# Attention by halves of the sequence: two head tiles at a time, column-tiled logits, and an output projection that starts inside the attention

## The chip, the cores and the metric

The kernel runs on one core of a Trainium2 chip. The core has a matrix engine (TensorE, PE in the profile), three elementwise engines (VectorE or DVE, ScalarE or ACT, GpSimd or POOL) and a queue engine (SyncE, SP) that starts transfers. Each engine executes its own instructions in order and waits on semaphores for the others. The time is the device time of one execution in microseconds; lower is better.

## The reference, cut to what matters

Two layers of attention and token MLP run one after the other on one sequence of 2048 positions and 1024 channels. The attention is local: every position looks at eight positions, itself and those 2, 4, ... 14 before it.

```python
def _A_ref(x, wqkv, wo):              # S = 2048, D = 1024, 32 heads of 32 channels
    W, dil = 8, 2
    q, k, v = ...                     # x @ wqkv, by heads
    idx = pos[:, None] - off[None, :] # off = 0, 2, ... 14; masked where idx < 0
    logits = einsum("bhsd,bhswd->bhsw", q, kg) * scale     # kg: k at idx
    attn = softmax(where(mask, logits, -1e9))
    o = einsum("bhsw,bhswd->bhsd", attn, vg)
    return o.reshape(B, S, D) @ wo

def _B_ref(x, w1, b1, w2, b2):        # mixes positions: 2048 -> 3584 -> 2048
    h = layernorm(x)
    u = gelu(einsum("bsd,sf->bdf", h, w1) + b1)
    return transpose(einsum("bdf,fs->bds", u, w2) + b2)

x = x + _A_ref(layernorm(x), wqkv, wo)
x = x + _B_ref(layernorm(x), w1, b1, w2, b2)
x = x + _A_ref(layernorm(x), wqkv, wo)
x = x + _B_ref(layernorm(x), w1, b1, w2, b2)
```

## The kernel before

One **unit** of the attention is one tile of 128 channels (four heads) over all 2048 positions, `t = 0..7`. Its steps are:

- `QK(t)` and `V(t)`: 64 and 32 matmuls of 512 columns; ScalarE copies the sums into `q_buf`, `k_buf`, `v_buf`.
- `products(t)`: VectorE multiplies q with the eight shifted copies of k, 8192 elements a partition for each half of the positions.
- `reduce(t)`: 32 matmuls with a 0/1 matrix `Z` sum the 32 channels of a head. All add into one PSUM tile `lg` of 128 partitions, each matmul filling four of them.
- `softmax1`, `softmax2`: VectorE and ScalarE; the weights go to DRAM (`attn_scr`) and come back spread over the channels (`bcast`, 2 MB for each half).
- `AVp`: VectorE multiplies them with the eight shifted copies of v; `accum` adds the eight, on VectorE, or on TensorE for the last two units.

```python
def reduce(t):
    lg = psum.tile([P, W, SUB], F32, name="lg", tag="lg", bufs=2)
    nc.tensor.matmul(lg[:CP], lhsT=maskL[:W, :], rhs=maskR[:W], start=True, stop=False)
    for hh in range(2):
        for jj in range(JH):
            j = hh * JH + jj
            nc.tensor.matmul(lg[:CP], lhsT=Z[:, ZOFF - H4 * j: ZOFF - H4 * j + CP],
                             rhs=pr_buf[hh][:, :, jj * SUB:(jj + 1) * SUB],
                             start=False, stop=(j == NJ - 1))

def pe_acc(t):
    return t >= ND - 2                     # ND = 8

for t in range(-2, ND + 1):                # a software pipeline over units
    AVp(t - 1, 0); accum(t - 1, 0)
    reduce(t); softmax1(t)
    ...                                    # AVp/accum of half 1, softmax2(t), bcast
    products(t + 1)
    QK(t + 2, ...); V(t + 1)
    load_wqkv(t + 3)
    if t + 1 == ND - 1:
        load_wo(); load_w1(0)
load_w1(1)
```

The output projection `OutProj.run` needs all eight units of a row. It follows the attention, 16 rows of 128 positions, each 16 matmuls, an addition of the residual on VectorE and the LayerNorm for the MLP; the first two rows are begun (seven of eight tiles) in the attention's last step.

```python
for i in range(NS):                        # NS = 16 rows
    self.mm(i, ...)                        # oh (attention out) x wo
    nc.vector.tensor_tensor(xo[:], pyv, xb[:], op=ALU.add)
    nc.sync.dma_start(self.xd[i * P:(i + 1) * P, :], xo[:])
    mv = ln_stats(xo[:])
    ...                                    # ScalarE writes the normalized row into oh
```

At the very start all 16 rows are normalized and transposed into `hT`; the attention begins with the last of them. In the second layer the second MLP step prepares `hT` while it runs.

Of the kernel before, what the change touches and what calls it, by code (L numbers as in the profile page):

```python
# [9 lines left out]
BF = mybir.dt.bfloat16  # L10
# [5 lines left out]
P = 128  # L16
# [8 lines left out]
NEG = -1.0e10  # L25


def build_kernel(ctx, tc, A_x, A_wqkv, A_wo, B_w1, B_b1, B_w2, B_b2, out, n_layers=2, dbg=None,
                 wq_eng="gpsimd"):
# [7 lines left out]
    NJ = S // SUB  # L37
    CP = NJ * H4
    assert CP <= P
    HS = S // 2  # L40
    JH = NJ // 2
    CPH = CP // 2
# [4 lines left out]
    wdma = {"gpsimd": nc.gpsimd, "sync": nc.sync, "scalar": nc.scalar}[wq_eng]  # L47
# [21 lines left out]
    maskR = const.tile([P, W, SUB], BF, name="maskR")  # L69
    eps_t = const.tile([P, 1], F32, name="eps_t")  # L70
# [3 lines left out]
    with tc.tile_pool(name="cbuild", bufs=1) as cb:  # L74
# [7 lines left out]
        mlf = cb.tile([P, CP], F32, name="mlf")  # L82
        nc.gpsimd.memset(mlf[:], 1.0)
        nc.gpsimd.affine_select(out=mlf[:], in_=mlf[:], pattern=[[-1, CP]],
                                compare_op=ALU.is_ge, fill=0.0, base=H4 - 1, channel_multiplier=0)
        nc.vector.tensor_copy(maskL[:], mlf[:])
# [29 lines left out]
    KT_W = HALO_PAD + S  # L116
# [3 lines left out]
    n_qkv = max(2 * S + 5 * KT_W, NF * 512)  # L120
    n_w = 2 * ND * 3 * P
    n_wv = 2 * ND * P
    n_wall = max(n_w + n_wv, NS * 512)
# [5 lines left out]
    R_w = R_wall[:, 0:n_w].rearrange("p (b k g c) -> p b k g c", b=2, k=ND, g=3)  # L129
    R_wv = R_wall[:, n_w:n_w + n_wv].rearrange("p (b k c) -> p b k c", b=2, k=ND)  # L130
# [11 lines left out]
    q_buf = [R_qkv[:, b * S:(b + 1) * S] for b in range(2)]  # L142
    k_buf = [R_qkv[:, 2 * S + b * KT_W: 2 * S + (b + 1) * KT_W] for b in range(2)]
    v_buf = [R_qkv[:, 2 * S + (2 + b) * KT_W: 2 * S + (3 + b) * KT_W] for b in range(3)]

    def zero_halos():
        for b in k_buf + v_buf:
            nc.vector.memset(b[:, 0:HALO_PAD], 0.0)
# [36 lines left out]
    def load_wqkv(t):  # L185
        if t < 0 or t >= ND:
            return
        b = t % 2
        with nc.allow_non_contiguous_dma("weight slice, 256B runs"):
            for g in range(3):  # L190
                nc.sync.dma_start(R_w[:, b, :, g, :], wq_view[:, :, g, t * P:(t + 1) * P])

    def permute_wv(t):
        if t < 0 or t >= ND:
            return
        b = t % 2
        nc.scalar.copy(R_wv[:, b, :, :].rearrange("p k (d h) -> p k d h", h=H4),
                       R_w[:, b, :, 2, :].rearrange("p k (h d) -> p k d h", h=H4))
# [19 lines left out]
    def attention(li, before_last_qk_chunk=None, drain_filler=None):  # L218

        def QK(t, hook=None):  # L220
            if t < 0 or t >= ND:
                return
            b = t % 2
            qT, kT = q_buf[b], k_buf[b]
            QW = min(1024, S)
            units = [(g, c2) for c2 in range(S // QW) for g in (0, 1)]
            for ui, (g, c2) in enumerate(units):
                if hook is not None and c2 == S // QW - 1 and g == 0:
                    hook()
                dst, off = (qT, 0) if g == 0 else (kT, HALO_PAD)  # L230
                pq = mm_tile()
                for n in range(QW // 512):
                    s0 = c2 * QW + n * 512
                    for kt in range(ND):
                        nc.tensor.matmul(pq[:, n * 512:(n + 1) * 512], lhsT=R_w[:, b, kt, g, :],  # L235
                                         rhs=hT[:, kt, s0:s0 + 512], start=(kt == 0), stop=(kt == ND - 1))
                nc.scalar.copy(dst[:, off + c2 * QW: off + (c2 + 1) * QW], pq[:, 0:QW])  # L237

        def V(t):
            if t < 0 or t >= ND:  # L240
                return
            b = t % 2
            vT = v_buf[t % 3]
            QW = min(1024, S)
            for c2 in range(S // QW):
                pq = mm_tile()
                for n in range(QW // 512):
                    s0 = c2 * QW + n * 512
                    for kt in range(ND):
                        nc.tensor.matmul(pq[:, n * 512:(n + 1) * 512], lhsT=R_wv[:, b, kt, :],  # L250
                                         rhs=hT[:, kt, s0:s0 + 512], start=(kt == 0), stop=(kt == ND - 1))
                nc.scalar.copy(vT[:, HALO_PAD + c2 * QW: HALO_PAD + (c2 + 1) * QW], pq[:, 0:QW])

        qkv_pitch = R_qkv.ap[0][0]

        def shifted(buf, col0):
            return bass.AP(buf.tensor, buf.offset + col0, [[qkv_pitch, P], [-DIL, W], [1, HS]])

        def products(t):
            if t < 0 or t >= ND:  # L260
                return
            qT, kT = q_buf[t % 2], k_buf[t % 2]
            for hh in range(2):
                nc.vector.tensor_tensor(pr_buf[hh], qT[:, hh * HS:(hh + 1) * HS].unsqueeze(1).to_broadcast([P, W, HS]),  # L264
                                        shifted(kT, HALO_PAD + hh * HS), op=ALU.mult)
# [3 lines left out]
        def reduce(t):  # L269
            if t < 0 or t >= ND:  # L270
                return
            lg = psum.tile([P, W, SUB], F32, name="lg", tag="lg", bufs=2)
            lg_tiles[t] = lg
            nc.tensor.matmul(lg[:CP], lhsT=maskL[:W, :], rhs=maskR[:W], start=True, stop=False)
            for hh in range(2):
                prod = pr_buf[hh]
                for jj in range(JH):
                    j = hh * JH + jj
                    nc.tensor.matmul(lg[:CP], lhsT=Z[:, ZOFF - H4 * j: ZOFF - H4 * j + CP],  # L279
                                     rhs=prod[:, :, jj * SUB:(jj + 1) * SUB],  # L280
                                     start=False, stop=(j == NJ - 1))

        sm_state = {}

        def softmax1(t):
            if t < 0 or t >= ND:
                return
            lg = lg_tiles.pop(t)
            mx = atp.tile([P, SUB], F32, name="mx")
            nc.vector.tensor_reduce(mx[:CP], lg[:CP].rearrange("p w s -> p s w"), axis=AX.X, op=ALU.max)  # L290
            lm = atp.tile([P, W, SUB], F32, name="lm")
            nc.vector.tensor_tensor(lm[:CP], lg[:CP], mx[:CP].unsqueeze(1).to_broadcast([CP, W, SUB]),
                                    op=ALU.subtract)
            nc.scalar.activation(lm[:CP], lm[:CP], ACT.Exp, scale=scale)
            sm_state[t] = lm

        def softmax2(t):
            if t < 0 or t >= ND:
                return None
            lm = sm_state.pop(t)  # L300
# [5 lines left out]
            scr = attn_scr[t % 2]  # L306
            with nc.allow_non_contiguous_dma("compact attn scatter, 128B runs"):
                for hh in range(2):
                    dst = bass.AP(scr.tensor, hh * H4 * W * HS, [[SUB, JH], [W * HS, H4], [HS, W], [1, SUB]])
                    nc.sync.dma_start(dst, at[hh * CPH:(hh + 1) * CPH])  # L310
                    if dbg is not None and "attn" in dbg and li == 0:
                        nc.sync.dma_start(bass.AP(dbg["attn"].tensor, t * H4 * W * S + hh * HS,
                                                  [[SUB, JH], [W * S, H4], [S, W], [1, SUB]]),
                                          at[hh * CPH:(hh + 1) * CPH])

            def bcast(hh):
                src = bass.AP(scr.tensor, hh * H4 * W * HS, [[0, DH], [W * HS, H4], [1, W * HS]])
                nc.sync.dma_start(ab_of(t, hh), src)

            bcast(0)  # L320
            return lambda: bcast(1)

        def ab_of(t, hh):
            return pr_buf[hh] if t == ND - 1 else ab_buf[hh]

        def AVp(t, hh):
            if t < 0 or t >= ND:
                return
            vT = v_buf[t % 3]
            ab = ab_of(t, hh)  # L330
            nc.vector.tensor_tensor(ab, ab, shifted(vT, HALO_PAD + hh * HS), op=ALU.mult)  # L331

        def pe_acc(t):
            return t >= ND - 2

        def accum(t, hh):
            if t < 0 or t >= ND:
                return
            ab = ab_of(t, hh)
            dst = oh[:, t, hh * HS:(hh + 1) * HS]  # L340
            if not pe_acc(t):
# [15 lines left out]
        zero_halos()  # L357
        for t in range(-2, ND + 1):
            AVp(t - 1, 0)
            accum(t - 1, 0)  # L360
            reduce(t)
            softmax1(t)
            if t == ND - 1:
                b1 = softmax2(t)
                b1()
                AVp(t - 1, 1)
                accum(t - 1, 1)
                if drain_filler is not None:
                    drain_filler()
            else:  # L370
                AVp(t - 1, 1)
                b1 = softmax2(t)
                accum(t - 1, 1)
                if b1 is not None:
                    b1()
            products(t + 1)
            if t + 2 >= 2:
# [234 lines left out]
```

## Time and profile before

| what | before |
|---|---|
| time, median of 4 runs | 1497.69 us (1497.25 to 1498.64) |
| span of the profiled run | 1495.8 us |
| start: LayerNorm and transposes | 0 to 46.4 us |
| attention of layer one, then of layer two | 46.4 to 330.5, and 771.7 to 1056 us |
| output projection | 330.5 to 377.9, and 1056 to 1104.4 us |
| MLP, two steps | 377.9 to 771.7, and 1104.4 to 1495.8 us |

The profile is a trace of one execution. A line of a group names the source line, the engine, the operation and its tiles (out<-in), and how often it ran; then its busy time and mean duration, and the idle time of the engine just before it with what ended it. The string of 40 digits gives the busy tenths of an engine in 40 equal slices of the span. L264 is the multiplication of `products`, L279 the matmuls of `reduce`, L331 the multiplication of `AVp`, L342 to L344 the additions of `accum` on VectorE, L353 those on TensorE, L413 the output projection, L459 and L494 the two MLP steps.

### The profile page before, as it was taken

How to read it: one execution, taken by the hardware profiler on the slowest of the kernel's cores; microseconds unless marked ns; L12 is line 12 of the kernel's file. 1: busy time of each engine (PE TensorE's matmuls, PEld its weight loads, DVE VectorE, ACT ScalarE, POOL GpSimd, SP SyncE). 2: the span in 40 equal slices, each digit the busy share in tenths (PEclk: the TensorE clock that was granted, in tenths of full speed). 3: DMA queues.
4: the chain of work that ended last, by engine and by line, in shares of the span. 5: the costliest groups of instructions: out<-in, count | busy, mean ns of one | idle time of the engine just before them, and what ended most of it. 6: DMA issues, size and time to landing. Idle time of an engine off the chain costs nothing.

```text
span 1495.8 us, 14782 instructions
## 1 busy us (share of the span) xinstructions
PE 1395.8 (93%) x6458; PEld 636.4 (43%) x6544; DVE 619.6 (41%) x633; ACT 326.8 (22%) x345; POOL 41.8 (3%) x53
## 2 busy tenths in 40 slices
PE   3999999489999999999999999965999999999998
PEld 2444444134444444444444444422444444444443
DVE  6439999758100001222234699995750000011111
ACT  4332232014211121222223332310441111100000
POOL 1000000100000000000000000010000000000000
PEclk9999999789999999999999999988999999999999
DMA  8134435864221333414111455286621311224410
GB/s 174 38 124 165 144 126 201 312 231 168 70 83 57 99 71 119 136 44 139 43 50 28 153 188 200 117 288 242 218 100 57 113 57 57 72 70 141 142 48 21
DMA packets 113857, 183.43 MB, mean 123 GB/s; under 512 B 75904, under 2 KB 75904, under 8 KB 109696
## 3 DMA queue, kind: packets, MB, share of 16 engines
q1 hardware_dynamic: 97824, 119.57, 24.0%
q0 software_dynamic: 15968, 62.92, 12.5%
q8 instruction: 51, 0.84, 0.2%
q14 instruction: 14, 0.11, 0.0%
HBM read 163.59 MB, written 18.87 MB: 122 GB/s over the span
## 4 chain that ended last, share of the span: by engine, by line
PE 73%; DVE 21%; DMA 4%; issue 1%; SPq 1%; ACT 0%; DVEq 0%; ACTq 0%
PE mm L459 26%; PE mm L494 26%; PE mm L235 7%; DVE R_att L331 7%; PE mm L413 6%; DVE R_att L264 5%; DVE R_att L342 3%; PE mm L250 3%; DMA R_att<-attn_scr 2%; PE lg L279 2%; PE mm L353 2%; DVE R_att L343 2%; DVE ln_stats L156 1%; DMA attn_scr<-at 1%; DVE sm L302 1%
## 5 line engine op out<-in xcount | busy, mean ns | idle before, releaser
L504 DVE SCALAR_TENSOR_TENSOR xo<-mm,b_sb,xb 128x1024 bf16<-128x1024 f32 x32 | 41.1, 1284 | 689.4 <-PE mm L494 689.4
L235 PE MATMUL mm<-R_hT,R_wall 128*128 128x512 bf16 x994 | 223.6, 381 | 1.7 <-issue 0.2
L459 PE MATMUL mm<-R_oh,R_hT 128*128 128x512 bf16 x1024 | 222.3, 379 | 0.0
L494 PE MATMUL mm<-R_att,R_oh 128*128 128x512 bf16 x878 | 194.1, 379 | 0.9
L494 PE MATMUL mm<-R_att,R_qkv 128*128 128x512 bf16 x876 | 193.8, 379 | 1.1
L264 DVE TENSOR_TENSOR R_att<-R_qkv 128x8192 bf16<-128x8192 bf16 x32 | 141.1, 4419 | 63.7 <-PE lg L279 43.1
L459 PE MATMUL mm<-R_oh,R_wall 128*128 128x512 bf16 x768 | 166.7, 379 | 0.0
L331 DVE TENSOR_TENSOR R_att<-R_att,R_qkv 128x8192 bf16<-128x8192 bf16 x32 | 141.4, 4418 | 47.8 <-DMA R_att<-attn_scr 47.8
L235 PEld LDWEIGHTS <-R_wall 128*128 128x128 bf16 x1024 | 100.6, 98 | 121.1 <-issue 2.2
L459 PEld LDWEIGHTS <-R_hT 128*128 128x128 bf16 x1024 | 100.1, 98 | 120.9
L279 PE MATMUL lg<-R_att,Z 128*128 128x512 bf16 x512 | 118.2, 388 | 30.7 <-DVE R_att L264 30.7
L494 PEld LDWEIGHTS <-R_qkv 128*128 128x128 bf16 x896 | 87.4, 98 | 104.3
L494 PEld LDWEIGHTS <-R_oh 128*128 128x128 bf16 x896 | 87.4, 98 | 103.8
L461 ACT ACTIVATE R_att<-mm,b_sb 128x1024 bf16<-128x1024 f32 x56 | 62.3, 1113 | 307.6 <-PE mm L459 307.5
L459 PEld LDWEIGHTS <-R_wall 128*128 128x128 bf16 x768 | 75.2, 98 | 90.6
L250 PE MATMUL mm<-R_hT,R_wall 128*128 128x512 bf16 x508 | 112.9, 379 | 0.2
L413 PE MATMUL mm<-R_hT,R_oh 128*128 128x512 bf16 x500 | 110.8, 379 | 1.1 <-ACT R_oh L355 0.5
L237 ACT CAST R_qkv<-mm 128x1024 bf16<-128x1024 f32 x64 | 64.7, 1011 | 194.8 <-PE mm L235 194.6
L279 PEld LDWEIGHTS <-Z 128*128 128x128 bf16 x512 | 50.0, 100 | 94.8 <-issue 40.3
L413 PEld LDWEIGHTS <-R_oh 128*128 128x128 bf16 x512 | 50.1, 98 | 61.2 <-issue 1.0
L250 PEld LDWEIGHTS <-R_wall 128*128 128x128 bf16 x512 | 50.1, 98 | 60.4
L353 PE MATMUL mm<-R_att,ident 128*128 128x512 bf16 x126 | 37.6, 462 | 30.3 <-DVE R_att L331 27.6
(65 smaller groups left out, 636.6 us busy)
## 6 DMA issues: line engine op xcount, KB each, us to landing
R_att<-attn_scr SPq DMA_DIRECT2D x32, 2048.0 KB, 9.6
R_hT<-in_B_w_dram POOLq DMA_DIRECT2D x8, 2048.0 KB, 9.6
R_qkv<-in_B_w_dram POOLq DMA_DIRECT2D x4, 3584.0 KB, 16.0
R_oh<-in_B_w_dram POOLq DMA_DIRECT2D x4, 3584.0 KB, 15.0
R_wall<-in_A_wqkv_dram SPq DMA_DIRECT2D x48, 256.0 KB, 3.1
R_wall<-in_B_w_dram POOLq DMA_DIRECT2D x6, 2048.0 KB, 9.5
x_scr<-xo SPq DMA_DIRECT2D x48, 256.0 KB, 2.2
xb<-x_scr SPq DMA_DIRECT2D x48, 256.0 KB, 3.2
```

The costliest lines, as they stand in the source:

```text
L235: nc.tensor.matmul(pq[:, n * 512:(n + 1) * 512], lhsT=R_w[:, b, kt, g, :], rhs=hT[:, kt, s0:s0 + 512], start=(kt == 0), stop=(kt == ND - 1))
L237: nc.scalar.copy(dst[:, off + c2 * QW: off + (c2 + 1) * QW], pq[:, 0:QW])
L250: nc.tensor.matmul(pq[:, n * 512:(n + 1) * 512], lhsT=R_wv[:, b, kt, :], rhs=hT[:, kt, s0:s0 + 512], start=(kt == 0), stop=(kt == ND - 1))
L264: nc.vector.tensor_tensor(pr_buf[hh], qT[:, hh * HS:(hh + 1) * HS].unsqueeze(1).to_broadcast([P, W, HS]), shifted(kT, HALO_PAD + hh * HS), ...
L279: nc.tensor.matmul(lg[:CP], lhsT=Z[:, ZOFF - H4 * j: ZOFF - H4 * j + CP], rhs=prod[:, :, jj * SUB:(jj + 1) * SUB], start=False, stop=(j == ...
L331: nc.vector.tensor_tensor(ab, ab, shifted(vT, HALO_PAD + hh * HS), op=ALU.mult)
L342: nc.vector.tensor_tensor(ab[:, 0:W:2, :], ab[:, 0:W:2, :], ab[:, 1:W:2, :], op=ALU.add)
L353: nc.tensor.matmul(po[:, n * CH:(n + 1) * CH], lhsT=ident[:], rhs=ab[:, w, c0:c0 + CH], start=(w == 0), stop=(w == W - 1))
L413: nc.tensor.matmul(py[:, d0:d0 + 512], lhsT=oh[:, t, i * P:(i + 1) * P], rhs=wo_sb[:, t, d0:d0 + 512], start=(t == 0), stop=(t == ND - 1))
L459: nc.tensor.matmul(pu[:, n * 512:(n + 1) * 512], lhsT=w1t[:, k, f4 * P:(f4 + 1) * P], rhs=h2_rhs(k, n * 512), start=(k == 0), stop=(k == N ...
L461: nc.scalar.activation(gT[:, ft, :], pu[:, 0:D], ACT.Gelu_apprx_tanh, bias=b1_sb[:, ft:ft + 1], scale=1.0)
L494: nc.tensor.matmul(py[:, n * 512:(n + 1) * 512], lhsT=w2t[:, k, s4 * P:(s4 + 1) * P], rhs=gT[:, k, n * 512:(n + 1) * 512], start=(k == 0), ...
```

## The change

The change makes a unit of **two** tiles over **half** of the positions: units 0 to 3 are the four pairs of tiles in the first half, units 4 to 7 the same pairs in the second. It has five parts.

1. The first four units need only the first eight rows of `hT`. The attention starts after these, and the other rows are normalized and transposed between its first projections (`pre_unit_hooks`).
2. The logits of units 0 and 1 are reduced inside the projections of the next unit (`early`), to start VectorE's chain sooner.
3. `reduce` uses column tiling: 32 matmuls with 32 columns each, on four column groups of the array, so that four may run side by side.
4. When unit 3 is done, the first half of the attention's output is complete. Its eight output rows are projected inside the last unit (`drain_filler`), with the residual added on TensorE by an identity matmul and the sum taken from PSUM by ScalarE (`act_evac`). Only the last unit's accumulation is left to TensorE.
5. The weights of Q and K have one buffer for a pair of tiles, loaded in runs of 512 bytes instead of 256. The first two w1 loads wait for the last unit (a two-element copy makes them do so). The 14 positions of k and v that the second half needs from the first are kept in a small `stash`.

```diff
+        def unit_tiles(U):
+            u, p = U % NU, U // NU
+            return p, (2 * u, 2 * u + 1)
...
-            nc.tensor.matmul(lg[:CP], lhsT=maskL[:W, :], rhs=maskR[:W], start=True, stop=False)
-            for hh in range(2):
-                    nc.tensor.matmul(lg[:CP], lhsT=Z[:, ZOFF - H4 * j: ZOFF - H4 * j + CP], ...
+                for r in range(8):
+                    for q in range(G):
+                        cp, j = q // gpc, (q % gpc) * 8 + r
+                        nc.tensor.matmul(lg[32 * q:32 * q + 32], lhsT=Z[:, ZOFF - H4 * r: ZOFF - H4 * r + 32],
+                                         rhs=pr_buf[cp][:, :, j * SUB:(j + 1) * SUB],
+                                         start=first[q], stop=(r == 7), tile_position=(0, 32 * q), ...)
...
-        def pe_acc(t):
-            return t >= ND - 2
+        def pe_acc(U, cp):
+            return U == NUNITS - 1
...
+            if t == NUNITS:
+                for b in range(2):
+                    nc.vector.tensor_copy(w1buf[b][:, 0, 0:2], ab_of(t - 1, 0)[:, 0, 0:2])
+                    load_w1(b)
...
+            if t == NUNITS - 1:
+                bc(1)
+                AVp(t - 1, 1)
+                drain_filler(0, nf // 2)
+                accum(t - 1, 1)
+                drain_filler(nf // 2, nf)
+                continue
...
+            if t + 2 == 1:
+                QK(1, inner=lambda: early(0), at=2)
+            elif t + 2 == 2:
+                QK(2, inner=lambda: early(1), at=0)
+            else:
+                QK(t + 2)
+            load_wqk(t + 3)
+            V(t + 1)
...
+                if act_evac:
+                    nc.tensor.matmul(py[:, d0:d0 + 512], lhsT=ident[:], rhs=xb[:, d0:d0 + 512],
+                                     start=True, stop=False)
...
+                if act_evac:
+                    nc.scalar.copy(xo[:], pyv)
+                else:
+                    nc.vector.tensor_tensor(xo[:], pyv, xb[:], op=ALU.add)
...
-        op.run()
+        attention(2 * l, pre_unit_hooks=hooks, drain_filler=lambda lo, hi, op=op: op.run(lo, hi, act_evac=True))
+        op.run(NS // 2, NS)
+        op.flush()
```

## The prediction

> **What bounds the kernel now.** I read the page's overall shares first, then the busy time by stretch, then VectorE's waits, then the groups of instructions.
>
> ```profile
> PE 1395.8 (93%) x6458; PEld 636.4 (43%) x6544; DVE 619.6 (41%) x633; ACT 326.8 (22%) x345; POOL 41.8 (3%) x53
> PE   3999999489999999999999999965999999999998
> DVE  6439999758100001222234699995750000011111
> ```
>
> PE (TensorE) looks like the bound of the whole kernel, but 93% is a mean over stages. DVE (VectorE) shows two humps of 9s where PE dips: the attention stages. The stretches, cut at the stage borders that the chain of waits gives (first attention from 46.4, its output projection from 330.5, the first MLP from 377.9 us), say:
>
> ```profile
> 46.40:138.00 91.60, 91.20 (x417) 41.36 (x424) 48.85 (x24) 28.86 (x29) 0.00 (x0) 1.00 0.27 81
> 138.00:296.00 158.00, 135.83 (x606) 59.97 (x614) 147.78 (x79) 37.61 (x36) 6.80 (x10) 0.95 0.58 212
> 296.00:330.50 34.50, 27.28 (x100) 11.00 (x103) 17.73 (x10) 5.79 (x6) 1.55 (x1) 0.82 0.50 187
> 330.50:377.90 47.40, 47.19 (x216) 21.52 (x220) 41.21 (x87) 21.23 (x29) 0.00 (x0) 1.00 0.54 188
> 377.90:571.60 193.70, 193.65 (x899) 87.76 (x898) 3.35 (x9) 38.39 (x35) 5.75 (x5) 1.00 0.24 71
> ```
>
> The columns are the stretch, its length, then busy us of PE, weight loads, DVE, ACT and POOL, then clock, DMA share, GB/s. So one attention has three parts: a start in which PE is full and DVE half idle (91.2 against 48.9 of 91.6 us); a middle in which DVE is full (147.8 of 158); a drain in which neither is (27.3 and 17.7 of 34.5). The output projection (47.4 us of PE) follows alone, then the MLP, pure PE. Over 46.4 to 330.5 DVE worked 48.9 + 147.8 + 17.7 = 214.4 of 284.1 us: 70 us idle in each attention, although DVE is its longest chain. What it waited for (the whole kernel, two attentions):
>
> ```profile
> DVE R_att L331 <- DMA R_att<-attn_scr: 47.8, 8, 11.7
> DVE R_att L264 <- PE lg L279: 43.1, 4, 18.8
> DVE R_att L264 <- ACT R_qkv L237: 20.5, 4, 9.8
> DVE mx L290 <- PE lg L279: 11.4, 2, 5.7
> ```
>
> The prices of DVE's and PE's work:
>
> ```profile
> L331 DVE TENSOR_TENSOR R_att<-R_att,R_qkv 128x8192 bf16<-128x8192 bf16 x32 | 141.4, 4418 | 47.8 <-DMA R_att<-attn_scr 47.8
> L264 DVE TENSOR_TENSOR R_att<-R_qkv 128x8192 bf16<-128x8192 bf16 x32 | 141.1, 4419 | 63.7 <-PE lg L279 43.1 <-ACT R_qkv L237 20.5
> L279 PE MATMUL lg<-R_att,Z 128*128 128x512 bf16 x512 | 118.2, 388 | 30.7 <-DVE R_att L264 30.7
> L342 DVE TENSOR_TENSOR R_att<-R_att 128x4096 bf16<-128x4096 bf16 x24 | 54.5, 2270 | 0.0
> L353 PE MATMUL mm<-R_att,ident 128*128 128x512 bf16 x126 | 37.6, 462 | 30.3 <-DVE R_att L331 27.6 <-ACT R_oh L355 2.2 <-issue 0.4
> ```
>
> A duration overlaps the next one's start a little, so I price by start-to-start distances in the timeline: product or attention-times-value 4.34, the accumulation of a half 2.20 + 1.13 + 0.60 = 3.93, a softmax 0.60 + 0.60 + 0.94 + 0.46 + 0.60 = 3.2 us. A unit is then 4 x 4.34 + 2 x 3.93 + 3.2 = 28.4, just the period in the middle (products start at 165.73, 193.65 and 222.60). PE's pitch is 0.216 us a matmul (896 in 193.39 us in the chain of waits, at the first MLP): Q and K of a unit (64) 13.8, V (32) 6.9, the logit reduction (32) 6.9, together 27.6: the two engines are balanced, so both must be relieved or rearranged.
>
> **What the Trainium skill says.** "TensorE: Matmul & The Clock Gate", section "Measured speedup vs the span model": matmuls on different column groups run at once; three of 32 columns and N = 512 gained 2.38 times. This trace has no such matmul. For four I take three times, an estimate from that page: 6.9 / 3 = 2.3, say 2.5 us. "DMA: Bandwidth & Descriptors", section "Anatomy of one DMA — SWDGE (gpsimd) path": DMA engines wait on no semaphore, the issuing sequencer does. The trace agrees: SP stood 163.6 us in L191 (the weight loads) for PE, so a load that waits holds up what SP issues after it. The first page, "What's actually happening": an idle TensorE falls to half its clock. Here the drain's clock was 0.82 and L353's matmuls averaged 462 ns against 379.
>
> **The change, part by part.** A unit was one head tile (128 channels) over all 2048 positions; it is two tiles over half the positions. Work per unit stays: 64 + 32 projection matmuls, two products, and so on. Order changes.
>
> 1. Start, first layer only. Q/K of unit 0 need rows 0 to 7 alone. The ninth normalization starts at 33.96 in the timeline and takes 0.53; its transposes follow, so Q/K start near 35.3, not at 46.4. The compiled order lets unit 0's first product go after one tile's Q and K (32 matmuls, the first ones cold, one transposed row between): about 46.6, against 55.47 now. Gain about 9 us on DVE.
>
> 2. The opening chain. The reduction of unit 0 sits inside unit 1's projections. Followed by hand in the compiled order: product 0b waits for K of the second tile (55.1); the single weight buffer is refilled after the last Q and K matmuls (256 KB took 3.1 us, so 512 KB about 4), unit 1's first tile is projected by 62.7; reduction 0 to 66.5; product 1a, softmax 0, product 1b to 80.5; attention weights 0 at 81.2. From there to the first attention-times-value the kernel before took 822.24 to 834.62 in its second attention, 12 us: 93. Unit 0's second broadcast and the buffer it shares put unit 1's at about 123. Of those 76 us DVE works 6 x 4.34 + 2 x 3.2 + 2 x 4.34 + 2 x 3.93 + 1 = 50 and idles 26.
>
> 3. The middle and drain on DVE, from 123: 14 attention-times-value (60.8), 10 products (43.4), 6 softmaxes (19.2), 12 accumulations (47.2; two more per layer than now, as only the last unit goes to PE), and the LayerNorm statistics of eight rows, moved in front of the last two multiplies: each 1.45 (a startup step of 1.845, L541 at 32.12 to 33.96, less 0.45 for the normalization), 11.6. Sum 182. I add 3 for broadcasts that land late: 308 us.
>
> 4. The drain on PE. Eight rows of the output projection, 18 matmuls each with the residual added by an identity matmul, 8 x 3.9 = 31 us, fill PE's gaps before 308. After it stand only: the last accumulation (16 matmuls, 3.5), half-clock after the idle time (+1.7), eight rows (128 x 0.216 = 27.6): the MLP starts at 341 instead of 377.9. Gain 37.
>
> 5. Second layer. No startup to hide; there the MLP starts 332.7 after the first Q/K (771.67 to 1104.37). Placing the same chain at a Q/K start of 771.67, attention weights 0 come after 39.3, and the MLP 81.2 - 39.3 = 41.9 earlier on that scale: 341 - 41.9 = 299 after. Gain 34.
>
> 6. ScalarE gets eight evacuations of 1.01 us a layer, same permutes in bigger pieces, small halo copies; with 29 busy of 92 us it has room. The MLPs are untouched.
>
> Sum: 37 + 34 = 71. Hand walks miss waits, as each of the 16 broadcasts shares its queue with weight loads; I take back 6 a layer. 1497.7 - 59 = 1439 us.
>
> **The rivals.** (a) Column groups do not run together: each reduction stays near 7 us. For it: no trace here shows them. Against: the page above. Three reductions lie in the opening chain, 4.5 us each; PE at 27.6 a unit would again match DVE: 12 a layer, 1463. (b) SP's queue becomes the new wait: the order puts a weight load that waits for PE, later the stores of projected rows, ahead of some broadcasts. For it: broadcasts took 7.1 to 14.0 us from issue to landing, and DVE already waits 47.8 for them. Against: most have 10 us or more of DVE work in front. Perhaps 4 to 10 a layer more than my allowance, 1450 to 1460. (c) The first MLP waits for its weights: on the software queue w2's 3.5 MB now stand before w1, both after the last multiply at 308. 16.0 + 9.6 us end near 335, six before the need; with row traffic beside it they could be up to 8 late: 1455. (d) The opening idles less than walked: if the 26 fell to 10, and nothing of the allowance were needed, 1395 to 1410. The order's own dependences speak against it.
>
> **Range and chances.** The floor of one layer is DVE's work: 231 us after 46.6, so some 25 us of idle is all that could still be won in each. (a) or (b) with (c) cost 20 to 25 in all. Hence 1439, 1418 to 1462 for 8 in 10. For less than 2% (above 1467.7) two rivals must come together: faster 0.93, within 2% 0.05, slower 0.02; slower needs a new wait of 90 us that nothing shows.
>
> **What would show it.** DVE's first product near 46.6; unit periods near 28.4 with DVE full from about 123 to 308; first MLP at about 341; second attention start to MLP about 299; a reduction's 32 matmuls in 2 to 3 us; DVE's waits for the reduction down to about half; PE busy some 79 us less (16 reductions x 4.5 = 72, and 64 accumulation matmuls at 0.216 = 14 gone, 32 identity matmuls = 7 new). Wrong would be: reductions of 7 us, a large wait for the broadcasts, or PE waiting on w1 at the MLP's first matmul.

## The result, and the profile after

| | before | after |
|---|---|---|
| time, median | 1497.46 us (13 runs) | 1421.05 us (8 runs, 1418.16 to 1422.49) |
| ratio, 95% interval | | 0.9491 [0.9481, 0.9500] |
| start of the first attention's products | 55.47 us | 47.56 us |
| first MLP starts at | 377.9 us | 335.5 us |
| second attention's first Q/K to its MLP | 332.7 us | 299.3 us |
| a step of the MLP (there are four) | 193.4 us | 193.4 us |

The change takes 76 us off: 42.4 before the first MLP and 33.4 in the second attention. The MLPs are what they were. In the changed kernel L311 is the multiplication of `products`, L335 the matmuls of `reduce`, L360 the first step of the softmax, L400 the multiplication of `AVp`, L412 the first addition of `accum` on VectorE, L423 its matmuls on TensorE, L275 and L298 the projections of Q/K and V, L280 the ScalarE copy of Q and K, L508 the output projection, L516 its residual addition on VectorE, L534 the first MLP step. The page of the changed kernel, busy time and tenths of PE and DVE:

```profile
PE 1304.3 (92%) x6423; PEld 593.2 (42%) x6512; DVE 615.1 (43%) x639; ACT 369.5 (26%) x389; POOL 41.8 (3%) x53
PE   2999988669999999999999998964999999999998
DVE  5779999974000002222226889999600000011111
```

DVE did the same work (615.1 against 619.6 us), PE 91 us less. PE still reads 92%, because the span shrank with it: the overall share tells nothing of what was won. The busy time by stretch, with the same columns as before, cut at the opening's end, the last multiplication and the MLP's first matmul:

```profile
37.80:118.30 80.50, 80.06 (x446) 37.58 (x454) 59.48 (x59) 38.79 (x45) 0.00 (x0) 1.00 0.45 146
118.30:302.20 183.90, 145.70 (x775) 63.24 (x788) 181.65 (x129) 67.27 (x71) 4.49 (x8) 0.91 0.61 219
302.20:335.50 33.30, 33.14 (x149) 14.99 (x151) 21.05 (x44) 12.73 (x16) 3.85 (x3) 0.98 0.91 325
335.50:529.20 193.70, 193.65 (x899) 87.76 (x898) 3.31 (x8) 41.47 (x35) 5.75 (x5) 1.00 0.23 73
```

Each stretch now has one full engine: PE in the opening (80.1 of 80.5 us), DVE in the middle (181.65 of 183.9), PE again in the drain (33.1 of 33.3). Before, the drain had no full engine and a separate projection of 47.4 us followed it. What DVE still waited for (both attentions):

```profile
DVE R_att L400 <- DMA R_att<-attn_scr: 18.8, 6, 5.5
DVE R_att L311 <- ACT R_qkv L280: 11.6, 4, 6.5
DVE R_att L311 <- PE lg L335: 10.2, 4, 4.5
DVE mx L360 <- PE lg L335: 4.9, 2, 2.7
```

The columns are us in total, times, longest. The wait for the broadcasts fell from 47.8 to 18.8 us, that for the reductions from 43.1 + 11.4 to 10.2 + 4.9. The groups, to be set beside those of before:

```profile
L400 DVE TENSOR_TENSOR R_att<-R_att,R_qkv 128x8192 bf16<-128x8192 bf16 x32 | 141.3, 4416 | 18.8 <-DMA R_att<-attn_scr 18.8
L311 DVE TENSOR_TENSOR R_att<-R_qkv 128x8192 bf16<-128x8192 bf16 x32 | 141.2, 4414 | 21.8 <-ACT R_qkv L280 11.6
L335 PE MATMUL lg<-R_att,Z 128*32 128x512 bf16 x512 | 38.8, 426 | 22.6 <-DVE R_att L311 22.6
L412 DVE TENSOR_TENSOR R_att<-R_att 128x4096 bf16<-128x4096 bf16 x28 | 63.8, 2278 | 0.1
L423 PE MATMUL mm<-R_att,ident 128*128 128x512 bf16 x63 | 19.7, 486 | 39.9 <-DVE R_att L400 39.8
```

The 512 matmuls of the reductions are as many as before and each is recorded no shorter than before (a mean of 426 ns; 388 then), but together they fill 38.8 us instead of 118.2. A mean duration therefore can't show that column groups overlap; the group's busy time can. The PE timeline at the end of the first attention (start, duration, then the idle time before it and its cause):

```profile
277.88 0.39 PE L329 MATMUL lg<-maskR,maskL 8*32 8x512 bf16 x2
297.95 9.96 PE L423 MATMUL mm<-R_att,ident 128*128 128x512 bf16 x32 [19.68 <-DVE R_att L400]
307.75 27.79 PE L508 MATMUL mm<-R_hT,R_oh 128*128 128x512 bf16 x125
335.38 4.91 PE L534 MATMUL mm<-R_oh,R_hT 128*128 128x512 bf16 x22
```

PE has finished its eight rows of output projection at 277.9 and waits 19.7 us for DVE; then the last accumulation, the other eight rows and the MLP follow without a gap.

### The profile page after: what moved, and what is told of

Read it like the earlier page. It is cut to its first block, busy times and chain, and to the rows that moved or that the text cites. A ratio compares the mean times of both kernels' runs of the same rounds, so it can differ in the third digit from the quotient of the medians.

```text
span 1420.0 us, 14694 instructions
## 1 busy us (share of the span) xinstructions
PE 1304.3 (92%) x6423; PEld 593.2 (42%) x6512; DVE 615.1 (43%) x639; ACT 369.5 (26%) x389; POOL 41.8 (3%) x53
## 4 chain that ended last, share of the span: by engine, by line
PE 68%; DVE 24%; DMA 4%; ACT 2%; issue 1%; another core or an unknown queue 0%; SPq 0%; DVEq 0%
PE mm L534 27%; PE mm L569 27%; DVE R_att L400 8%; DVE R_att L311 6%; PE mm L275 6%; PE mm L508 4%; DVE R_att L412 3%; DMA R_att<-attn_scr 2%; DVE R_att L413 2%; DVE ln_stats L162 2%; PE mm L298 1%; PE mm L423 1%; PE mm L181 1%; DVE sm L376 1%; DVE R_oh L414 1%
## 5 line engine op out<-in xcount | busy, mean ns | idle before, releaser
L275 PE MATMUL mm<-R_hT,R_wall 128*128 128x512 bf16 x992 | 225.8, 381 | 4.2 <-DMA R_wall<-in_A_wqkv_dram 2.2
L534 PE MATMUL mm<-R_oh,R_hT 128*128 128x512 bf16 x1024 | 222.3, 379 | 0.0
L534 PE MATMUL mm<-R_oh,R_wall 128*128 128x512 bf16 x768 | 166.7, 379 | 0.0
L275 PEld LDWEIGHTS <-R_wall 128*128 128x128 bf16 x1024 | 99.0, 98 | 125.7 <-issue 8.8
L534 PEld LDWEIGHTS <-R_hT 128*128 128x128 bf16 x1024 | 100.2, 98 | 120.8
L311 DVE TENSOR_TENSOR R_att<-R_qkv 128x8192 bf16<-128x8192 bf16 x32 | 141.2, 4414 | 21.8 <-ACT R_qkv L280 11.6
L400 DVE TENSOR_TENSOR R_att<-R_att,R_qkv 128x8192 bf16<-128x8192 bf16 x32 | 141.3, 4416 | 18.8 <-DMA R_att<-attn_scr 18.8
L508 PE MATMUL mm<-R_hT,R_oh 128*128 128x512 bf16 x499 | 113.2, 379 | 2.6 <-DMA R_hT<-in_A_wo_dram 1.9
L298 PE MATMUL mm<-R_hT,R_wall 128*128 128x512 bf16 x508 | 113.0, 379 | 0.2
L534 PEld LDWEIGHTS <-R_wall 128*128 128x128 bf16 x768 | 75.1, 98 | 90.6
L508 PEld LDWEIGHTS <-R_oh 128*128 128x128 bf16 x512 | 49.8, 98 | 64.8 <-issue 6.0
L298 PEld LDWEIGHTS <-R_wall 128*128 128x128 bf16 x512 | 49.9, 98 | 60.5 <-issue 0.6
L185 ACT CAST R_hT<-mm 128x1024 bf16<-128x1024 f32 x32 | 32.2, 1013 | 123.4 <-PE mm L181 123.4
L412 DVE TENSOR_TENSOR R_att<-R_att 128x4096 bf16<-128x4096 bf16 x28 | 63.8, 2278 | 0.1
L216 ACT COPY R_wall<-R_wall 128x2048 bf16<-128x2048 bf16 x16 | 59.4, 3714 | 15.6 <-DMA R_wall<-in_A_wqkv_dram 15.6
L162 DVE BATCH_NORM_STATS2 ln_stats<-xo 128x6 f32<-128x512 bf16 x96 | 61.4, 677 | 1.1
## 6 DMA issues: line engine op xcount, KB each, us to landing
R_hT<-in_B_w_dram POOLq DMA_DIRECT2D x8, 2048.0 KB, 10.4
R_wall<-in_B_w_dram POOLq DMA_DIRECT2D x6, 2048.0 KB, 10.6
```

What stands on the lines that cost most here:

```text
L162: nc.vector.bn_stats(out=stats[:, i, :], in_=xr[:, i, :])
L216: nc.scalar.copy(R_wv[U % 2].rearrange("p k c (d h) -> p (k c) d h", h=H4), R_wvs.rearrange("p k c (h d) -> p (k c) d h", h=H4))
L275: nc.tensor.matmul(pq[:, n * CHK:(n + 1) * CHK], lhsT=R_wqk[:, kt, g, cp, :], rhs=hT[:, kt, s0:s0 + CHK], start=(kt == 0), stop=(kt == ND ...
L298: nc.tensor.matmul(pq[:, n * CHK:(n + 1) * CHK], lhsT=wv[:, kt, cp, :], rhs=hT[:, kt, s0:s0 + CHK], start=(kt == 0), stop=(kt == ND - 1))
L311: nc.vector.tensor_tensor(pr_buf[cp], qb[:, cp, :].unsqueeze(1).to_broadcast([P, W, HS]), shifted(kb[:, cp, :]), op=ALU.mult)
L400: nc.vector.tensor_tensor(ab, ab, shifted(v_buf[U % 3][:, cp, :]), op=ALU.mult)
```

## The experiments

Twelve kernels: six undo one part of the change, three add to it, two put one part alone into the kernel before, one changes only an order. Times are medians; a difference is taken from 1421.05 us, the changed kernel. Beside these runs the kernel before had medians of 1495.85 to 1497.93 us, so 2 us between two runs mean nothing. The unit of two tiles over half the positions, on which the other parts rest, and the weight loads in runs of 512 bytes were not undone alone. An edit can also change the order in which the compiled program puts the instructions of an engine; where a trace shows this, it is said.

**Column tiling undone.**

```diff
-    coltile=True
+    coltile=False
```

> The changed kernel with the reduction on the whole array again (each of its 32 matmuls fills 128 PSUM partitions), all else kept. Theory A (the gain is the new order: projection in the drain, VectorE's chain started earlier; column tiling only shortens the opening chain): a reduction goes from 1.9 back to 7 us, three of them lie one after the other in the opening while TensorE is full there, later VectorE's 28.4 us a unit still covers TensorE's 27.7; 12 to 15 us a layer, so 1445 to 1451 us. Theory B (the gain is TensorE's relief by column tiling): most of the 76 us go, 1470 us or more.

1447.8 us (1446.87 to 1448.63), ratio 0.9666 [0.9652, 0.9681]: 27 us slower, theory A. The reductions' matmuls fill 116.8 us of PE again, and DVE waits 43.1 us for broadcasts instead of 18.8. The third reduction and the multiplication that depends on it:

```profile
132.34 7.08 PE L348 MATMUL lg<-R_att,Z 128*128 128x512 bf16 x32
161.71 4.43 DVE L400 TENSOR_TENSOR R_att<-R_att,R_qkv 128x8192 bf16<-128x8192 bf16 x1 [11.09 <-DMA R_att<-attn_scr]
```

Here L348 is the reduction. The third one ends at 139.4 us instead of 124.3, three times 5 us later, as theory A had it. Its softmax then starts at 142.0 instead of 131.3, and DVE waits 11.1 us for the broadcast (12.2 at the same place in the second layer): what comes late out of a reduction goes late to the softmax and comes late back. DVE's order differs too: two products that the changed kernel has done before this multiplication come after it here. The MLP starts 14.2 us later in the first layer, and the second adds 11.0.

**Column tiling alone, in the kernel before**, four groups in turn over both halves:

```diff
-for hh in range(2):
-    for jj in range(JH): ...                          # one group of 128 columns
+for r in range(8):
+    for q in range(4):
+        hh, jj = q // 2, (q % 2) * 8 + r
+        nc.tensor.matmul(lg[32*q:32*q+32], lhsT=Z[:, ZOFF-H4*r: ZOFF-H4*r+32],
+                         rhs=pr_buf[hh][:, :, jj*SUB:(jj+1)*SUB], tile_position=(0, 32*q), ...)
```

> The kernel before with column tiling in its reduction and nothing else of the change. Theory A: three reductions of 5 us in each opening, where TensorE is full, and some of VectorE's 5.7 us wait for the last reduction; 13 to 18 us a layer, so 1461 to 1471 us, less than half of the 76 us. Theory B: TensorE's relief is the change; 1440 us or less.

1500.77 us, ratio 1.0016 [1.0007, 1.0024]. Both theories were wrong: the part that is worth 27 us in the changed kernel is worth nothing by itself. DVE's waits in this run:

```profile
DVE R_att L264 <- PE lg L281: 80.4, 14, 17.1
DVE R_att L335 <- DMA R_att<-attn_scr: 24.6, 8, 6.3
```

Here L281 is the reduction, L264 and L335 are the multiplications of `products` and `AVp`. The wait for the broadcasts is halved as hoped (47.8 before), but the products wait 80.4 us for reductions, in 14 places; before it was 43.1 in 4. The suspicion: in this loop the first matmuls already touch both product buffers, so the reduction can't run on the first half alone and gives back neither buffer before its end. PE's timeline shows the stop:

```profile
128.03 0.39 PE L281 MATMUL lg<-R_att,Z 128*32 128x512 bf16 x2
135.50 1.90 PE L281 MATMUL lg<-R_att,Z 128*32 128x512 bf16 x30 [0.93 <-DVE R_att L264]
```

Only the two matmuls in front of the first one on the second buffer run early; the other 30 come after the second product.

**The same, half by half**: only the order of the same 32 matmuls differs.

```diff
-for r in range(8):
-    for q in range(4):
+for hh in range(2):
+    for r, q in [(r, 2*hh + g) for r in range(8) for g in range(2)]:
```

> The kernel before with column tiling, but half by half: the 16 matmuls of the first half on two column groups, then those of the second half on the other two. The first try with all four groups interleaved took 1500.8 us; there VectorE waited 80 us for the reduction, against 54 before. Theory E (interleaving the halves made every reduction need both products before it goes on and free both buffers only at its end, and this wait ate the gain): the wait falls below 45 us and the time to 1462 to 1478 us. Rival (a shorter reduction is worth nothing here, since broadcasts and the drain set the time): 1492 us or more.

1475.11 us, ratio 0.9861 [0.9846, 0.9875]: the order alone is worth 25.7 us (23 when each run is compared with the kernel before beside it).

```profile
DVE R_att L264 <- PE lg L281: 54.9, 4, 17.1
DVE R_att L335 <- DMA R_att<-attn_scr: 18.8, 8, 5.6
```

Four waits are left, all in the openings (17.1 and 10.3 us in each); the ten others are gone. The suspicion holds. The time is in the range that theory E gave, but the wait of the products for reductions fell only to 54.9 us, not below 45, and is above the 43.1 of before: what fell below its value there is the wait for the broadcasts (18.8 instead of 47.8), and the last multiplication of layer one ends 8.2 us earlier (314.6 against 322.8).

**The changed kernel with that order.**

```diff
-for r in range(8):
-    for q in range(G):
+for hh in range(2):
+    for r, q in [(r, hh * gpc + g) for r in range(8) for g in range(gpc)]:
```

> The changed kernel with its column-tiled reductions run half by half (two column groups at a time, on the same half of the heads) instead of four groups in turn over both halves. In the kernel before, that order alone made 25.7 us of difference (1500.8 against 1475.1), because a reduction over both halves frees both product buffers only at its end. If the early reductions and their hooks of the changed kernel already take that wait away (its DVE waits for reductions sum to only 10.2 + 4.9 us, all in the openings), the order makes no difference here: 1417 to 1425. Rival: two groups instead of four run side by side, so each reduction takes twice as long, 3.7 us instead of 1.85, and the DVE order in the drain shifts: 1427 to 1440. Third: the first half's buffer comes free sooner, also in the openings: 1405 to 1416.

1423.05 us (1419.95 to 1424.21), ratio 0.9503 [0.9489, 0.9518]: no difference. The reductions take longer (56.6 us of PE in all, not 38.8), and no time is lost by it. So what makes four groups in turn harmless here is not the loop but the order of units around it; which part of that, no run separates.

**Early reductions undone**: `reduce` after the whole of QK and V of the next unit.

```diff
-    QK(1, inner=lambda: early(0), at=2)
+    QK(1)
-    QK(2, inner=lambda: early(1), at=0)
+    QK(2)
```

> The changed kernel without the early reductions: units 0 and 1 are reduced in their ordinary place, after the V projection that follows. Theory A (the opening chain on VectorE sets everything after it): reduction 0 ends 14 us later, and with it the next product, which needs the buffer that the reduction reads; 10 to 14 us a layer, 1441 to 1449 us. Rival (the opening is bound by TensorE's projections and the weight loads, which stay as they are): 4 us or less in all, 1425 us or below.

1436.21 us, ratio 0.9601 [0.9586, 0.9615]: 15 us slower, between the two theories. DVE's timeline in the opening of that run:

```profile
54.74 4.42 DVE L311 TENSOR_TENSOR R_att<-R_qkv 128x8192 bf16<-128x8192 bf16 x1 [2.00 <-ACT R_qkv L280]
...
78.12 4.42 DVE L311 TENSOR_TENSOR R_att<-R_qkv 128x8192 bf16<-128x8192 bf16 x1 [18.80 <-PE lg L335]
...
100.71 4.43 DVE L311 TENSOR_TENSOR R_att<-R_qkv 128x8192 bf16<-128x8192 bf16 x1 [9.60 <-PE lg L335]
105.06 4.42 DVE L400 TENSOR_TENSOR R_att<-R_att,R_qkv 128x8192 bf16<-128x8192 bf16 x1
```

The third product starts at 78.1 instead of 64.5, the first attention-times-value at 105.1 instead of 89.7: 15.4 us later. The last multiplication is only 9.4 later (307.3 against 297.9). The rest came back in waits: the broadcasts, started earlier than DVE gets to them, are waited for 1.2 us in the whole run instead of 18.8. Here the engine that started late found its inputs ready.

**All sixteen rows projected after the attention.**

```diff
-attention(2 * l, ..., drain_filler=lambda lo, hi, op=op: op.run(lo, hi, act_evac=True))
-op.run(NS // 2, NS)
+attention(2 * l, ..., drain_filler=None)
+op.run(0, NS)
```

> The changed kernel with all 16 rows of the output projection after the attention, residual added on VectorE as before; half-sequence units, early start and column tiling kept. Theory A: eight rows of 3.45 us come back behind the attention (27.6 a layer), against which the last multiplies no longer stand behind 11.6 us of LayerNorm statistics, of which the last broadcasts give back at most 7; 20 to 24 us a layer, 1461 to 1469 us. Theory C (the projection in the drain is mostly paid back by the statistics that it puts on VectorE's path): 10 us a layer or less, 1441 us or below.

1456.98 us, ratio 0.9730 [0.9715, 0.9744]: 36 us slower, the largest part of the change; at 18 us a layer it lies between theory A (20 to 24) and theory C (10 or less). Its drain on PE:

```profile
289.88 9.05 PE L423 MATMUL mm<-R_att,ident 128*128 128x512 bf16 x32 [19.50 <-DVE R_att L400]
298.77 55.42 PE L508 MATMUL mm<-R_hT,R_oh 128*128 128x512 bf16 x256
```

Per layer: 27.6 us more projection behind the accumulation, but the accumulation ends 9 us earlier (298.8 against 307.75). So the eight rows in the drain save 27.6 and cost about 9. Most of that is on DVE, whose last multiplication ends at 294.7 here and at 302.3 with the rows' LayerNorm statistics in front of it.

**The rows in the drain evicted by DVE as before**, not by an identity matmul and ScalarE.

```diff
-drain_filler=lambda lo, hi, op=op: op.run(lo, hi, act_evac=True)
+drain_filler=lambda lo, hi, op=op: op.run(lo, hi, act_evac=False)
```

> The changed kernel with the eight output rows in the drain evicted as before, by one DVE addition from PSUM, without the residual matmuls on PE and the copy on ACT (the order of the rows is unchanged). Theory (part 4's eviction by ACT keeps DVE free where DVE sets the end): 8 x 2 additions per layer fall between the last units' multiplies on a DVE that is full; 16 additions of about 0.7 us are 11 us a layer, less the residual matmuls on PE that lie beside it anyway: 8 to 11 us a layer slower, 1437 to 1443. Rival: DVE has waits for broadcasts and for the rows' own chain there that the additions fill: under 4 us a layer, 1421 to 1429.

1441.41 us (1439.95 to 1443.0), ratio 0.9626 [0.9610, 0.9642]: 20 us slower, as expected. DVE's timeline:

```profile
294.26 4.42 DVE L400 TENSOR_TENSOR R_att<-R_att,R_qkv 128x8192 bf16<-128x8192 bf16 x1
298.59 2.35 DVE L516 TENSOR_TENSOR xo<-mm,xb 128x1024 bf16<-128x1024 f32 x2
303.37 1.21 DVE L516 TENSOR_TENSOR xo<-mm,xb 128x1024 bf16<-128x1024 f32 x1
305.83 1.21 DVE L516 TENSOR_TENSOR xo<-mm,xb 128x1024 bf16<-128x1024 f32 x1
308.68 4.42 DVE L400 TENSOR_TENSOR R_att<-R_att,R_qkv 128x8192 bf16<-128x8192 bf16 x1
```

The eight additions (one of 1.2 us a row, not two of 0.7 as the expectation had it) lie in front of the last multiplication, which starts 10.8 us later than at 297.9. The PE and ScalarE work that replaced them lies in idle time.

**Late start**: all sixteen rows of `hT` before the first Q and K. The second layer is untouched.

```diff
-        if i == NH - 1:
-            break
+        pass
...
-    hooks = {0: [pull_one] * min(4, rest), 1: ...}
+    hooks = {}
+    rest = 0
```

> The changed kernel with all 16 rows normalized and transposed before the first projection, as before; the second layer is untouched. Theory A: VectorE's first product moves from 47.6 to about 56 us and everything after it by as much; 8 to 9 us, so 1429 to 1430 us. Theory D (the opening is bound by TensorE and weight loads, and the transposes put between its projections cost what the start gains): 3 us or less, 1421 to 1424 us.

1432.79 us, ratio 0.9566 [0.9552, 0.9580]: 11.7 us slower, theory A in kind, but 3 us above its range. The first product moves from 47.56 to 57.71, by 10.2 us where 8.4 were expected, and all of that shows at the first MLP, which starts at 345.6 instead of 335.4. The broadcasts don't absorb it.

**w1 not held back**: the two-element copies out, the loads behind the projection's weights and behind the loop.

```diff
-    if t == NUNITS:
-        for b in range(2):
-            nc.vector.tensor_copy(w1buf[b][:, 0, 0:2], ab_of(t - 1, 0)[:, 0, 0:2])
-            load_w1(b)
...
         load_wo()
+        load_w1(0)
...                                     # behind the loop
+load_w1(1)
```

> The changed kernel with the first 4 MB of the MLP's weights (w1) no longer held back by the two-element copies: the first half is requested right after the projection's weights, the second behind the loop. Theory F (the hold-back of part 5 does work): the loads meet the scatter and the broadcasts of the last units on the same DMA engines, which the last multiply and the accumulation wait for (the changed kernel's DVE waits for broadcasts sum to 18.8 us), so each layer loses 4 to 10 us: 1429 to 1441 us; the summed wait of DVE for broadcasts rises above 25. Rival: the broadcasts aren't in the way of anything any more, because 5 to 10 us lie between landing and use: within 4 us of the changed kernel, 1417 to 1425.

1430.13 us (1428.39 to 1430.96), ratio 0.9552 [0.9538, 0.9567]: 9 us slower, the size that theory F named, but not by its cause: DVE waits 20.3 us for broadcasts, hardly more than 18.8. The chain of waits of that run shows the other cause, and GpSimd's timeline where it comes from (L506 is here the output projection):

```profile
225.23 3.14 PE mm L298 x14
228.37 0.07 issue
228.44 7.36 DMA R_hT<-in_A_wo_dram
235.79 0.04 issue
235.84 3.42 PE mm L506 x9
239.26 2.15 PE lg L335 x23
```

```profile
222.87 1.17 POOL L230 DMA_DIRECT2D R_wall<-in_B_w_dram  x1 [75.73 <-PE mm L298]
228.44 2.16 POOL L222 DMA_DIRECT2D R_hT<-in_A_wo_dram  x4 [4.40 <-PE mm L298]
```

The compiled program does not keep the order of the text: one half of w1 (2 MB, into `R_wall`, the half that the text has behind the loop) was issued at 222.9, ahead of the last four of wo's eight pieces. The first of these needs 7.4 us to land; PE, whose first projected row needs it, stands idle for 4.5, and the reduction that follows in PE's order starts at 239.2 instead of 231.5. The softmax on DVE waits 2.3 us for it and 1.7 more for ScalarE. The Trainium skill, "DMA: Bandwidth & Descriptors", section "Two DMAs through the same engine are not ordered", says that within one queue of an engine descriptors start in order; that fits wo behind w1, though no run here puts w1 on another queue. In the changed kernel these four pieces are issued at 225.8 with nothing of w1 ahead of them, and PE waits 0.7 us. PE's waits for wo in the whole run: 11.2 us here, 1.9 there.

**Two additions.** First, the statistics of output rows 4 to 7 behind the last two multiplications, where DVE has idle time:

```diff
-    mv = ln_stats(xo[:])
-    self.flush()
-    rs, nb = ln_rs_nb(mv, double=True)
-    self.prev = (i, xo, rs, nb)
+    if act_evac and i >= NS // 4:
+        self.late.append((i, xo))       # normalized by norm_late() after the attention
+    else:
+        self.norm(i, xo)                # the four lines above
```

> The changed kernel with the LayerNorm statistics of output rows 4 to 7 put after the last unit's two multiplies instead of before them. Theory A (VectorE's order sets the end of the attention; the first of the last two broadcasts lands about 8 us before its multiply starts): the multiplies start 5.8 us earlier and TensorE's last accumulation with them; 5 to 6 us a layer, 1409 to 1412 us. Rival (the last broadcast sets the end): 2 us a layer or less, 1417 us or more.

1408.46 us (1407.21 to 1410.13), ratio 0.9415 [0.9401, 0.9429]: 12.6 us faster, half a us better than the range. The last multiplication of layer one ends at 296.7 instead of 302.3, 5.6 us earlier, where 5.8 were expected.

Second, one half of the accumulations from unit 2 on moved from DVE to PE:

```diff
-    return U == NUNITS - 1
+    return U == NUNITS - 1 or (cp == 1 and U >= 2)
```

> The changed kernel with the second tile's accumulation of units 2 to 6 on TensorE (16 identity matmuls, 3.45 us, and one ScalarE copy) instead of VectorE (3.93 us). Theory A (VectorE alone is full in the middle, TensorE has 28.4 - 22.6 = 5.8 us a unit to spare since column tiling): up to 5 x 3.9 us off VectorE's chain a layer, of which 8 to 16 stay, so 1389 to 1405 us. Rival (in-order TensorE then waits for the multiply before each accumulation, and the projections behind it come late): 1415 us or more.

1408.34 us (1407.78 to 1412.08), ratio 0.9422 [0.9406, 0.9437]: 12.7 us faster, less than expected. DVE works 19.4 us less between 118.3 and 302.2 (162.29 against 181.65), but its waits for broadcasts rise to 34.1 us, and the drain's last projected row stands in front of the accumulation on PE. That row is itself late, as it waits for its residual from DRAM:

```profile
288.20 0.61 PE L503 MATMUL mm<-xb,ident 128*128 128x512 bf16 x2 [4.12 <-DMA xb<-in_A_x_dram]
```

L503 begins a row with its residual, by the identity matmul. The last accumulation starts at 293.8, behind this row; DVE's last multiplication had ended at 291.6. No run here tests an earlier load of that residual.

**Both together.**

> Two edits that each gained some 13 us by themselves, together: the accumulation of every second half on PE from unit 2 on (1408.3 us alone), and the statistics of output rows 4 to 7 behind the last two multiplies (1408.5 us alone). If they shorten different parts of the same DVE queue, they add: 1421 - 12.7 - 12.6 = 1396, range 1393 to 1400. Rival: with the accumulation gone from DVE it already waits for the broadcasts at the end, so that moving the statistics only turns busy time into wait: 1403 to 1409.

1406.58 us (1405.8 to 1412.23), ratio 0.9405 [0.9384, 0.9425]: the rival. The two don't add; with either one alone or with both the time is the same within the intervals. The busy time from 250 to 300 us, first of the changed kernel, then of this one:

```profile
250.00:300.00 50.00, 23.40 (x111) 9.25 (x113) 50.00 (x60) 16.29 (x21) 0.00 (x0) 0.70 0.61 230
```

```profile
250.00:300.00 50.00, 46.84 (x230) 20.22 (x229) 42.69 (x51) 19.97 (x25) 3.86 (x3) 0.96 0.78 283
```

In the changed kernel DVE is busy all 50 us and PE 23.4. With both edits DVE has 7 us idle and PE 3: PE has nearly become the full engine, and its last row (to 295.4) stands in front of the accumulation. What DVE was relieved of came back as 36.2 us of waiting for broadcasts. These three are the fastest versions measured, 87 to 90 us below the kernel before.

## Why the prediction was right, and where it was off

1439 was predicted, 1421.05 measured: inside the range, 3 us above its lower end, with a gain of 76 us instead of 59. The path and most prices were right; the waits were put too high in sum. Point by point:

1. *Start, Q/K near 35.3, first product at 46.6:* 37.0 and 47.56. Gain 7.9 of 9. Undone, it costs 11.7.
2. *Opening: attention weights 0 at 81.2, first attention-times-value 93, unit 1's 123; DVE works 50 of 76 us:* 77.7, 89.7, 118.3; DVE works 51.5 of 70.75. The work was right and the idle time 19 instead of 26. Of the 4.7 us, 2.0 lie at the first reduction: the walk lets it end 3.8 us after the projection before it (62.7 to 66.5, although its own price of 2.5 gives 65.2); it took 1.9, and product 1a started at 64.47. Another 1.5 lie between there and the attention weights, and 1.4 between the first attention-times-value and unit 1's.
3. *Middle and drain on DVE, 182 us of work and 3 of waits, end at 308:* 181.65 us of work in 183.9, end at 302.3. The count of DVE's instructions by their start-to-start distances came out within half a microsecond, and the unit period of 28.4 was 28.36 (multiplications at 193.47, 221.83 and 250.19). One price was added wrongly: 1.845 less 0.45 is 1.40 for a row's statistics, not 1.45, so 11.2 a layer and not 11.6. Moving half of them gained 5.6 us on DVE in layer one.
4. *Drain on PE, 3.5 + 1.7 + 27.6 after the last multiplication, MLP at 341:* 5.5 to the start of the eight rows, 27.7 for them, MLP at 335.5. The sum was 32.8 and is 33.3; all of the 5.5 us gained against 341 came from steps 2 and 3.
5. *Second layer, 299:* 299.3. Here the end is right by luck, since two errors cancel: unit 1's attention-times-value came 4.3 us before the walk's place (76.8 after the first Q/K, not 81.1) and the stretch from there to the last multiplication's end took 189.5 us instead of 185.
6. *ScalarE has room:* its busy time went from 326.8 to 369.5 and DVE waits 11.6 us for its copies before the first products and 6.6 us for the exponentials of the softmax (20.5 and 2.9 before).

The term that was mis-sized is **the allowance of 6 us a layer for missed waits**. The walks without it gave 71; the trace gives 42.4 + 33.4 = 75.8. In layer one nothing of it was needed, and the walk itself was 5 us too long; in layer two the middle was 4.5 us longer than walked, and the opening, 4.3 shorter, had already paid for it.

The rivals: (a) *column groups not concurrent, 1463*: refuted in the trace, and the price of 12 a layer was close, 27 us for both when tiling was undone. (b) *A new wait in SP's queue*: the wait for broadcasts fell to 18.8. (c) *w1 late*: its first half was issued at 304.4 and landed 21.5 us later, at 325.9, 9.5 before the MLP; its second half landed at 333.8 and is first used at 363.0. (d) *An opening that idles only 10*: it idles 19. Of the signs named, *reductions in 2 to 3 us* were 1.9, *the waits for reductions down to half* were down to 28% (15.1 of 54.5 us), and PE was 91 us less busy instead of 79, mainly because the reductions fell by 79.4 instead of 72 and the accumulations on PE by 18 instead of 14.

What the prediction didn't see, though its time doesn't depend on it: the parts don't add. Undone one at a time they cost 36 (rows in the drain), 27 (column tiling), 15 (early reductions), 12 (start) and 9 (w1 held back), together 99 us for a gain of 76, and tiling alone in the kernel before gains nothing in the change's order of matmuls, 21 us half by half.

## What to carry to other kernels

Name the full engine of each stretch and count its instructions by start-to-start distances: where an engine was full here the count was good to half a microsecond, and an allowance on top of it for unnamed waits was the error. Before packing matmuls that read several buffers, look at which buffer each order frees first: the same 32 matmuls in two orders were 25.7 us apart in one schedule and equal in another. Work that fills the idle time of one engine may be paid for on another that serves it, as the eight rows were with 7.6 us of DVE, so ask what each filler puts in front of the chain's last instruction, and expect two cures for the same queue to overlap rather than add.

## What the runs showed of the hardware

- Four column groups of 32 columns ran nearly side by side: 32 matmuls in 1.91 us against 7.07 before, 3.7 times. After idle time, at the lower clock of the drain (a mean of 0.70 from 250 to 300 us), 30 of them took 3.60 us. The Trainium skill, "TensorEngine Tiling (Array Packing)", section "Theoretical Speedup", gives up to four times for a dimension of 32; the trace comes close to it.
- A transfer's landing time depends on what is ahead of it: such 2 MB loads had a median of 10.4 to 10.6 us from issue to landing over the whole run, but the two of w1 at the first MLP, issued right behind 3.5 MB of w2 on the same queue, needed 21.5 and 28.2.
